# One core, attention and a gated MLP: the calls of a kernel kept in a list and issued in the order of a list schedule made in the kernel

## The chip, the cores and the metric

The kernel runs on one core of a Trainium2 chip. The metric is the device time of one execution in microseconds (us). Three runs of the kernel before took 531.16, 533.72 and 533.61 us, median 533.61 us. One more execution, the profiled one, took 530.32 us, and every row of the profile is from it.

The core has five engines that run side by side, each in the order of its own queue: TensorE (PE, matrix products; its weight loads are shown apart as PEld), VectorE (DVE), ScalarE (ACT), GpSimd (POOL) and SyncE (SP), which here only issues transfers (DMAs). An instruction starts when its engine has come to it and the semaphores that it waits for are set. So the order of the queues decides which wait ends where.

## The reference

The input is `q`, `k`, `v` of shape (4 batches, 8 heads, 768 rows, 64), and four arrays of an MLP: `w_in` (512, 1024), `w_spatial` (768, 768), `b_spatial` (768), `w_out` (512, 512). The three MLP matrices but for `w_spatial` come as 64-bit floats.

```
scores = scale * q @ k^T                              # 768 x 768 for each head
keep   = (column < n_global) or (0 <= row - column < n_local)      # 8 and 96
bias   = -slope[h] * distance                         # n_local for a far global column
a      = softmax(where(keep, scores + bias, -1e9));   a /= sum + 1e-9
x      = (a @ v), heads side by side                  # 4 x 768 x 512
h      = relu(x @ w_in);   u, v = halves of h         # 512 features each
v_n    = (v - mean(v)) / sqrt(var(v) + 1e-6)          # over the features of a row
v_s    = w_spatial @ v_n + b_spatial                  # over the 768 rows of a batch
out    = (u * v_s) @ w_out
```

Since only 96 columns to the left and 8 global ones are kept, a block of 128 rows needs two blocks of 128 columns, its own and the one before it; the global columns are put into a corner of the latter that is masked otherwise.

## The kernel before

**Steps and tokens.** The work of attention goes in 24 steps n = 0 to 23, six for each batch (b = n // 6, i = n % 6), each of 128 rows and all eight heads. Around the steps stand pieces of other work, named by tokens of a letter and two digits in a table `CFG['S']` (batch 0) or `CFG['T']` (the later batches). The letters:

- P, `prep`: transfers of q and k. In batch 0 they land straight in their places (L279, L280). From batch 1 on they are loaded into `qkraw` (L294), split into a rounded high part and the rest (L127, L123), and copied by twelve further transfers from there into `q`, `ql` and `kring` (L302, L303, L300), so that one product of 128 rows takes both parts.
- S, `scores`: for each pair of heads a product (L364 in batch 0 in plain 32-bit floats, L367 afterwards in two passes of split parts), bias and row minimum on DVE (L373), exponent on ACT (L377), reciprocal of the sums (L259, L260), and the scaling of the 128x256 probabilities on POOL (L388).
- A, `values`: transposes on PE (L421), copies or splits out of the transposes' PSUM (L50, L127, L123), the product with v (L430, from batch 1 L451), and the assembly and split of x into `xth` and `xtl` (L50, L461, L463, L127, L123). W, `prep_v`: loads and splits v.
- V, `mlp_v`: half of x @ w_in for 128 rows (L493), relu, mean and variance, and the split into `vnh` and `vnl`. U, `mlp_u`: the other half for 256 rows (L516, L517). G, `mlp_s`: the product with `w_spatial` for 256 rows (L531), plus b and times u (L533, L535), split into `gh` and `gl`. O, `mlp_o`: the product with `w_out` (L549), the copy out of PSUM (L50) and the output transfer (L551). A product of the MLP and of the later attention is made in three passes of high and low parts.
- I, Q, T, B: the set-up of `w_in` (eight tiles of 128x512), `w_out` (four), `w_spatial` (six, L242) and b. A tile of the 64-bit weights is loaded as words (L197), turned into a 32-bit float and a rest by an ACT instruction (L222) and six of DVE (L223 to L228), and split by two of POOL (L230, L231) and one of ACT.

The second digit of a token is the tile, the first is by how many batches the token lags behind the step: V15 in batch 1 is the last V of batch 0. After the last step come V15, U12, then by hand G for chunk 0, G for chunk 1 (its result in the places of `xth` and `xtl`, which are free by then), O 0, G 2, O 1, O 2.

**What sets the order.** The kernel is written in one run from top to bottom. The framework's own scheduler (the program is built with `schedule_with_timeline_sim=True`) moves instructions between the tokens and fixes the order of each queue. Tiles come from pools with rotating buffers. Of the tiles that matter below, `qkraw`, `qkhi`, `q` and `ql` have one buffer each, `kring` two columns, the probabilities `pr` ten buffers, `pth` two, `vnh` and `vnl` six each, `gh` and `gl` one each; the weight set-up takes its two intermediates from the `vnh` and `vnl` buffers and its words from the three of `u`. In PSUM the scores, the transposes and the MLP have two places each, the product with v one of two banks.

Of the kernel before, what the change touches and what calls it, by code (L numbers as in the profile page):

```python
# [23 lines left out]

CFG = {'bpos': 1, 'v0pos': 0, 'bias1': 'pppppppp', 'bias2': 'pppppppp', 'S': [['P', 'I01', 'S', 'W', 'A', 'I00'], ['P', 'S', 'W', 'T01', 'T00', 'A', 'V00', 'B00'], ['P', 'S', 'V01', 'Q00', 'Q01', 'W', 'U00', 'A'], ['V02', 'P', 'W', 'T04', 'S', 'T03', 'A'], ['P', 'S', 'W', 'A'], ['P', 'A', 'T02', 'Q02', 'V04', 'V03', 'S', 'W', 'Q03', 'T05', 'U01']], 'T': [['P', 'W', 'A', 'V15', 'U12', 'S'], ['P', 'A', 'S', 'G10', 'W'], ['P', 'W', 'A', 'S', 'O10', 'V00'], ['G11', 'P', 'A', 'S', 'V01', 'O11', 'W'], ['P', 'W', 'A', 'U00', 'G12', 'V02', 'S'], ['P', 'W', 'U01', 'A', 'S', 'V03', 'V04', 'O12']], 'END': ['V15', 'U12'], 'lead': {}, 'pre_n': 1, 'pre0': 0, 'pre1': 1, 'whi': 'a', 'wsub': 'p', 'wadd': 'p', 'wth': 'a', 'wtl': 'p', 'vhi': 'p', 'vlo': 'p', 'qhi': 'a', 'qlo': 'v', 'khi': 'a', 'klo': 'v', 'pth0': 'aaaa', 'x0h': 'aa', 'x0l': 'vv', 'pth': 'aaaa', 'xh': 'aa', 'c1': 'aa', 'xl': 'pppp', 'vnh': 'a', 'vnl': 'p', 'gm': 'pp', 'gh': 'aa', 'gl': 'pv', 'o': 'aa', 'norm0': 'pppppppp', 'norm': 'pppppppp', 'dup': 1, 'fold': '', 'xb': 1, 'div': 'a', 'rows': 'p', 'xf0h': 'a', 'xf0l': 'v', 'xdiv': 'v', 'xbh': 'a', 'xbl': 'p', 'b_rawqk': 1, 'b_ev': 3, 'b_raw': 1, 'b_pr': 10, 'b_pth': 2, 'b_c1': 3, 'b_ps_s': 2, 'b_ps_p': 2, 'b_ps_o': 2, 'b_ps_m': 2}
NLMAX = 97

# [713 lines left out]
```

## Time and profile before

| | |
|---|---|
| median of three runs | 533.61 us (531.16 to 533.72) |
| the profiled execution | 530.32 us, its span 528.5 us |
| busy PE / DVE / POOL / ACT | 474.2 / 350.6 / 325.4 / 301.9 us |
| matmuls | 3116 |
| mean granted TensorE clock | 0.97 |
| moved by DMA | 65.50 MB, 124 GB/s on average |

The profile's span starts with the first instruction and ends with the last; 1.8 us of the profiled execution lie around it. Busy times count an instruction's own duration. Matmuls overlap each other in the array, so their busy time is more than the time that they take from start to start, and a busy PE may still be slower than it could be. The chain of waits follows the work that ended last back through whatever released each step. In a row of the timeline or of a group, brackets or arrows name what ended the idle time before the instruction.

### The profile page before, as it was taken

To read this page: it belongs to the slowest core of one execution; us is meant where nothing else is said; L and a number is where in the kernel's file an instruction comes from. 1 tells how busy PE (TensorE), PEld (TensorE's weight loads), DVE (VectorE), ACT (ScalarE), POOL (GpSimd) and SP (SyncE) were. 2 spreads that over 40 slices of the span, in tenths; PEclk is the share of its full clock that TensorE was granted. 3 is DMA by queue.
4 is the path that set the end of the run, shared out by engine and by line. 5 is a ranking of instruction groups with operands and counts; after the bars stand their busy time and mean duration, and the time that the engine had idled before them with its cause. 6 is when DMAs were issued, how large, how long until landed. Compare 5 with 4: busy or idle time off the path is not lost.

```text
span 528.5 us, 9830 instructions
## 1 busy us (share of the span) xinstructions
PE 474.2 (90%) x3116; PEld 427.9 (81%) x3116; DVE 350.6 (66%) x972; ACT 301.9 (57%) x800; POOL 325.4 (62%) x450
## 2 busy tenths in 40 slices
PE   3757599898988999997989999989999999979994
PEld 2535489678977999986979899969989899869994
DVE  6899988869697585476785775767587856331210
ACT  3775478666666484666575575675475576431111
POOL 6999997866774753846662947644753757523320
PEclk9987789999999999999999999998999999989998
DMA  7993412961755755466655764655755760000002
GB/s 173 288 245 106 144 60 52 214 145 51 153 139 138 172 133 125 98 154 160 145 118 150 169 163 99 147 146 137 159 112 147 183 140 21 22 20 1 21 35 73
DMA packets 68269, 65.50 MB, mean 124 GB/s; under 512 B 6672, under 2 KB 49936, under 8 KB 68208
## 3 DMA queue, kind: packets, MB, share of 16 engines
q1 hardware_dynamic: 68208, 64.78, 49.9%
q8 instruction: 27, 0.44, 0.4%
q14 instruction: 34, 0.28, 0.2%
HBM read 29.76 MB, written 6.68 MB: 69 GB/s over the span
## 4 chain that ended last, share of the span: by engine, by line
PE 48%; DVE 17%; DMA 13%; SPq 8%; ACT 6%; issue 5%; POOL 2%; DVEq 0%; ACTq 0%; POOLq 0%
PE sps L531 13%; PE vps L493 8%; PE ups L516 8%; PE ops L549 7%; PE ops L451 4%; DVE pr L373 3%; PE pt L421 3%; DMA qkraw<-in_k_dram 3%; PE sp L367 3%; ACT pr L377 2%; DMA qkraw<-in_q_dram 2%; DMA kring<-qkraw 2%; SPq L303 2%; DVE qkraw L123 2%; SPq L300 2%
## 5 line engine op out<-in xcount | busy, mean ns | idle before, releaser
L388 POOL TENSOR_SCALAR pr<-pr,rc 128x256 f32<-128x256 f32 (+1 forms) x192 | 99.6, 537 | 23.4 <-DVE rc L260 9.1
L377 ACT ACTIVATE pr<-pr,mn 128x256 f32<-128x256 f32 (+1 forms) x192 | 92.2, 482 | 33.7 <-DVE mn L373 32.5
L421 PE MATMUL pt<-ident,pr 128*128 128x128 f32 x352 | 58.4, 280 | 14.7 <-POOL pr L388 11.6
L373 DVE CUSTOM_DVE_ANT_0 pr<-sp,bias 128x256 f32<-128x256 f32 (+1 forms) x192 | 68.1, 395 | 4.6 <-PE sp L364 1.4
L421 PEld LDWEIGHTS pt<-ident,pr 128*128 128x128 f32 x352 | 42.0, 143 | 23.9 <-POOL pr L388 16.5
L123 DVE TENSOR_TENSOR pth<-pt,pth 128x512 fp32r<-128x512 f32 (+1 forms) x72 | 46.0, 642 | 16.6 <-ACT pth L127 15.4
L535 POOL TENSOR_TENSOR g<-g,u 128x512 f32<-128x512 f32 x24 | 32.0, 1331 | 34.8 <-DVE g L533 34.7
L127 ACT ACTIVATE pth<-pt 128x512 fp32r<-128x512 f32 (+1 forms) x72 | 39.2, 558 | 23.6 <-PE pt L421 20.9
L123 POOL TENSOR_TENSOR xtl<-c,xth 128x256 fp32r<-128x256 f32 x36 | 27.3, 758 | 35.8 <-ACT xth L127 28.5
L123 POOL TENSOR_TENSOR vnl<-vr,vnh 128x512 fp32r<-128x512 f32 x24 | 31.9, 1332 | 27.6 <-ACT vnh L127 26.6
L531 PE MATMUL sps<-w_t_l,vnh 128*128 128x256 f32 x288 | 45.8, 286 | 0.0
L531 PE MATMUL sps<-w_t_h,vnh 128*128 128x256 f32 x288 | 44.9, 286 | 0.8 <-ACT u L517 0.5
L451 PE MATMUL ops<-pth,vring 128*128 128x256 f32 x264 | 41.8, 288 | 3.0 <-DVE pth L123 2.1
L461 DVE TENSOR_TENSOR c<-ops,c 64x256 f32<-64x256 f32 x72 | 30.3, 421 | 21.4 <-ACT c L50 16.6
L531 PE MATMUL sps<-w_t_h,vnl 128*128 128x256 f32 x288 | 44.4, 285 | 0.0
L364 PE MATMUL sp<-kring,q 128*128 128x256 f32 (+1 forms) x96 | 28.7, 450 | 16.8 <-DMA kring<-in_k_dram 9.9
L451 PEld LDWEIGHTS ops<-pth,vring 128*128 128x128 f32 x264 | 36.4, 192 | 5.2 <-DVE pth L123 2.8
L367 PE MATMUL sp<-kring,q 128*128 128x256 f32 (+1 forms) x144 | 38.3, 292 | 2.4 <-DMA q<-qkhi 1.2
L531 PEld LDWEIGHTS sps<-w_t_h,vnh 128*128 128x128 f32 x288 | 38.7, 191 | 1.6 <-ACT vnh L127 0.8
L531 PEld LDWEIGHTS sps<-w_t_l,vnh 128*128 128x128 f32 x288 | 39.0, 191 | 0.0
L533 DVE TENSOR_TENSOR g<-sps,b_bc 128x512 f32<-128x512 f32 x24 | 16.5, 686 | 33.8 <-PE sps L531 31.5
L531 PEld LDWEIGHTS sps<-w_t_h,vnl 128*128 128x128 f32 x288 | 38.6, 191 | 0.0
(115 smaller groups left out, 1204.4 us busy)
## 6 DMA issues: line engine op xcount, KB each, us to landing
q<-qkhi SPq DMA_DIRECT2D x72, 128.0 KB, 2.5
ql<-qkraw SPq DMA_DIRECT2D x72, 128.0 KB, 2.5
out_dram<-o SPq DMA_DIRECT2D x23, 256.0 KB, 2.6
qkraw<-in_q_dram SPq DMA_DIRECT2D x36, 128.0 KB, 3.0
qkraw<-in_k_dram SPq DMA_DIRECT2D x36, 128.0 KB, 2.9
raw<-in_v_dram SPq DMA_DIRECT2D x18, 256.0 KB, 3.2
kring<-qkhi SPq DMA_DIRECT2D x36, 128.0 KB, 2.5
kring<-qkraw SPq DMA_DIRECT2D x36, 128.0 KB, 2.5
```

Source lines behind the costliest of these rows:

```text
L123: e_lo.tensor_tensor(out=lo, in0=src, in1=hi.bitcast(F32), op=ALU.subtract)
L127: nc.scalar.activation(hi, src, AF.Copy)
L367: nc.tensor.matmul(sp[:, j], lhsT=a[:, g, j] if CFG["dup"] else a[:, h], rhs=kring[:, h, sl], start=(y == 0), stop=(y == 1))
L373: nc.vector.tensor_tensor_reduce(out=pr, in0=sp[:, j], in1=bt, scale=-scale, scalar=3e38, op0=ALU.add, op1=ALU.min, accum_out=mn[:, h:h + 1],)
L377: nc.scalar.activation(pr, pr, AF.Exp, bias=mn[:, h:h + 1], scale=-1.0, accum_out=sm[:, h:h + 1])
L388: nc.gpsimd.tensor_scalar(out=pr, in0=pr, scalar1=rc[:, h:h + 1], scalar2=1.0, op0=ALU.mult, op1=ALU.mult)
L421: nc.tensor.transpose(pt[:, c, j], probs[2 * g + j][:, c * P:(c + 1) * P], ident)
L451: nc.tensor.matmul(ops[:, j], lhsT=vring[:, order[c], g, 2 * j:2 * j + 2].rearrange("p x d -> p (x d)"), rhs=pth[:, 2 * c + j].rearrange(" ...
L493: nc.tensor.matmul(ps, lhsT=a[:, t, toks], rhs=w[:, t, FH:], start=(x == 0), stop=(x == len(passes) - 1))
L516: nc.tensor.matmul(ps[:, j], lhsT=w[:, t, f * P:(f + 1) * P], rhs=a[:, t], start=(x == 0), stop=(x == len(passes) - 1))
L531: nc.tensor.matmul(ps[:, j], lhsT=vn[b, s][x][:, f * P:(f + 1) * P], rhs=w[:, s, ts_], start=(y == 0), stop=(y == len(passes) - 1))
L549: nc.tensor.matmul(ps[:, cs], lhsT=a[:, f, x * P:(x + 1) * P], rhs=w[:, f, cs], start=(y == 0), stop=(y == len(passes) - 1))
```

## The change

The products, their number, shapes and passes, and the work of each token are those of before. Changed is how the order comes about, and where tiles lie.

**Recording.** `nc` is replaced by a `Recorder` whose engines do not issue a call but keep it (`Op`), with its token and a number. At the end `plan()` sorts them, and they are issued in that order under `tc.manual_schedule()`, which turns the framework's scheduler off. All instructions now carry the line of `Op.issue`, L35, so that they are told apart by the names of their places.

**The list schedule.** `link()` finds for each call the earlier ones whose buffers overlap its own. `cost()` gives each a duration and a time to its result by formulas. `plan()` lets the five engines run by these: an engine that becomes free takes, of the calls that are ready, the one with the lowest rank. The rank is the token's: n for values, n + 0.2 for the loads and splits of step n + 1, n + 0.5 for its scores and for every MLP token in step n; at equal rank the call written earlier comes first. POOL's instructions and the DVE instructions that touch no PSUM are never run at the same time in it.

**Places.** Instead of rotating buffers, `Slots` hands out fixed places in turn. The weight set-up's intermediates now lie in `raw0`, `raw1`, `rawh0`, `rawh1`, which are also the only places of `qkraw` and `qkhi`, and the words of `w_out` in `gh` and `gl`.

**Tokens.** `scores` and `values` are written in two halves of four heads, taken alternately (a half of A for step n, a half of S for step n + 1, and again). The table is new, and END is `V05 U02 G00 O00 G01 O01 G02 O02`, without the spare places for the second `gh` and `gl`. The constant 1e-9 that is added to the sums is put into a second column beforehand, and a `tensor_reduce` takes the place of the `tensor_scalar` (L259).

```diff
+class Engine:
+    def __getattr__(self, call):
...
+        def keep(*args, **kw):
+            self.rec.add(self, call, args, kw)
...
+def cost(op):
+    n = elements(op.writes[0])
...
+    if op.eng == "sync":
+        size = n * 4 * list(op.writes[0].ap)[0][1]
+        return 560, 2200 + size * .0035, False
...
+def plan(ops, keys, trace=None):
+    link(ops)
...
+    rank = [(keys.get(op.token[0], op.token[1]), op.num) for op in ops]
+    free = {x: 0.0 for x in ("tensor", "vector", "scalar", "gpsimd", "sync")}
...
+        x = heapq.heappop(ready[e])[1]
...
+        start[x] = t
+        free[e] = t + op.busy
+        end = t + op.late
...
+            at = t + op.busy if o.eng == e and e != "sync" else end + SLACK
+            est[s] = max(est[s], at)
...
+    return sorted(ops, key=lambda op: (start[op.num], op.num))
+
+BUFS = {"gh": 1, "gl": 1, "u": 3, "s": 2, "p": 2, "m": 2, "raw0": 1, "raw1": 1, "rawh0": 1, "rawh1": 1}
+SLACK = 200
...
-        c = work.tile([P, w], F32, name="wc", tag="vnh", bufs=6)
+        c = work.tile([P, w], F32, name="wc", tag=("raw0", "rawh0")[x % 2])
-        a = work.tile([P, w], F32, name="wa", tag="vnl", bufs=6)
+        a = work.tile([P, w], F32, name="wa", tag=("raw1", "rawh1")[x % 2])
...
-        split_weights(w_out[t * P:(t + 1) * P], w_out_h[:, t], w_out_l[:, t])
+        split_weights(w_out[t * P:(t + 1) * P], w_out_h[:, t], w_out_l[:, t], ("gh", "gl")[t % 2], t)
...
     def recip(out, sums):
-        nc.vector.tensor_scalar(out=out, in0=sums, scalar1=1e-9, scalar2=None, op0=ALU.add)
+        nc.vector.tensor_reduce(out=out, in_=sums, op=ALU.add, axis=mybir.AxisListType.X)
...
-    def mlp_s(b, c, tags=(("gh", 1), ("gl", 1))):
+    def mlp_s(b, c):
...
+            if tok == "A":
                 if more:
+                    nc.token(("P", n + 1), n + .2)
+                    qq = prep(n + 1)
+                    s = scores(n + 1, qq)
+                a = values(n)
+                for x in range(2):
+                    steps("A", a, n)
+                    if more:
+                        steps("S", s, n + 1)
...
+    for tok in CFG["END"]:
+        run(tok, B * NB, B - 1, int(tok[2]))
+    nc.off()
+    with tc.manual_schedule():
+        for op in plan(nc.ops, KEYS):
+            op.issue()
```

The token tables, before and now:

```
before S [P I01 S W A I00] [P S W T01 T00 A V00 B00] [P S V01 Q00 Q01 W U00 A] [V02 P W T04 S T03 A] [P S W A] [P A T02 Q02 V04 V03 S W Q03 T05 U01]
       T [P W A V15 U12 S] [P A S G10 W] [P W A S O10 V00] [G11 P A S V01 O11 W] [P W A U00 G12 V02 S] [P W U01 A S V03 V04 O12]
now    S [I01 A] [I00 T00 T01 A V00 B00] [T02 T03 A V01 U00] [T04 T05 A V02] [Q00 Q01 A V03 U01] [Q02 Q03 A V04]
       T [V15 U12 A] [G10 O10 A] [G11 O11 A] [G12 O12 V00 V01 U00 A] [V02 A] [V03 U01 A V04]
```

**What moves on SP, at the border of batch 0 and batch 1.** Before, SP's queue has the twelve copies for step 6 (`q`, `ql` and `kring` out of `qkhi` and `qkraw`) ahead of the last two tiles of `w_out`:

```order
L302 DMA q_1029<-qkhi 64x512 x4
L480 DMA vring_223<-in_v_dram 32x512
L325 DMA vring_223<-in_v_dram 128x512
L303 DMA ql<-qkraw 64x512 x4
L300 DMA kring<-qkhi 64x4x128
L300 DMA kring<-qkraw 64x4x128
L300 DMA kring<-qkhi 64x4x128
L300 DMA kring<-qkraw 64x4x128
L197 DMA wst<-in_moe_w_out_dram 128x1024 x2
```

Now, with q in `q_0_151` and `q_0_152` and the loads of q and k in `raw_0_114` and `raw_0_115`:

```order
L35 DMA gh_130<-in_moe_w_out_dram 128x1024
L35 DMA gl_131<-in_moe_w_out_dram 128x1024
L35 DMA raw_0_114<-in_q_dram 64x4x128 x2
L35 DMA vg<-vring_155 32x1024
L35 DMA raw_156<-in_v_dram 128x512
L35 DMA raw_0_115<-in_k_dram 64x4x128 x2
L35 DMA q_0_151<-rawh_0_153 64x512 x4
L35 DMA q_0_152<-raw_0_114 64x512 x4
L35 DMA kring_150<-rawh_0_154 64x4x128 x2
L35 DMA kring_150<-raw_0_115 64x4x128 x2
```

The last two words of `w_out` have moved ahead of all that belongs to step 6, its loads and its copies.

**What moves on PE, at the same border.** Before, the scores of step 6 (`sp`, from `kring` and `q` or `ql`) are in front of the first products with v of step 5, batch 0's last (`ops` from `pth_1060`):

```order
L367 MATMUL sp<-kring,q_1029 128x128
L367 MATMUL sp<-kring,ql 128x128
L421 MATMUL pt<-ident,pr 128x128 x8
L493 MATMUL vps<-w_in_h,xth 128x512 x2
L493 MATMUL vps<-w_in_l,xth 128x512 x4
L493 MATMUL vps<-w_in_h,xtl 128x512 x2
L430 MATMUL ops<-pth_1060,vring_223 128x256 x2
L430 MATMUL ops<-pth_1069,vring_223 128x256 x2
```

Now the products of step 5 (`ops_93`) are followed by MLP work of batch 0 (`m_132`, `m_140`: what is left of V04, then V15, U12 and the first of G10):

```order
L35 MATMUL ops_93<-pth_123,vring_112 128x256 x2
L35 MATMUL ops_93<-pth_125,vring_112 128x256 x2
L35 MATMUL m_132<-w_in_h,xtl_121 128x512 x3
L35 MATMUL m_140<-w_in_h,xth_120 128x512 x4
L35 MATMUL m_140<-w_in_l,xth_120 128x512 x4
L35 MATMUL m_140<-w_in_h,xtl_121 128x512 x4
L35 MATMUL m_132<-xth_120,w_in_h 128x256 x4
L35 MATMUL m_132<-xtl_121,w_in_h 128x256 x4
```

The first scores of step 6 (`s_102`, `s_105`) come 15 matmuls of 512 columns, 48 of U and ten of G behind the last product with v:

```order
L35 MATMUL m_140<-w_t_h,vnh_148 128x256
L35 MATMUL m_140<-w_t_h,vnh_158 128x256
L35 MATMUL s_102<-kring_150,q_0_151 128x128
L35 MATMUL s_102<-kring_150,q_0_152 128x128
L35 MATMUL s_105<-kring_150,q_0_151 128x128
L35 MATMUL s_105<-kring_150,q_0_152 128x128
L35 MATMUL m_132<-w_t_h,vnh_160 128x256
```

So the scores of step 6 have moved from ahead of batch 0's last values to well behind them.

More of the change, by code (lines that the diff above doesn't have):

```diff
@@ L2 @@
+import heapq
 from contextlib import ExitStack
@@ new lines, with __init__, tile @@
+class Slots:
+    def __init__(self, pool, words, bufs):
+        self.pool, self.words, self.bufs, self.have, self.turn = pool, words, bufs, {}, {}
+    def tile(self, shape, dtype, name=None, tag=None, bufs=None):
+        tag = tag or name
+        bufs = self.bufs.get(tag, bufs or 2)
+        n = 1
+        for x in shape[1:]:
+            n *= x
+        x = self.turn.get(tag, 0)
+        self.turn[tag] = x + 1
+        place = f"{tag}_{x % bufs}"
+        key = place, dtype == F32R
+        if key not in self.have:
+            t = self.have[key] = self.pool.tile([P, self.words.get(tag, n)], F32, name=place, tag=place)
+            places[t[:].tensor.name] = place
+        t = self.have[key][:, 0:n]
+        if dtype != F32:
+            t = t.bitcast(dtype)
+        dims = " ".join("abcdef"[:len(shape) - 1])
+        return t if len(shape) == 2 else t.rearrange(f"p ({dims}) -> p {dims}", **dict(zip("abcdef", shape[1:])))
@@ new lines, with extent @@
+SIZE = {BF16: 1}
+seen = {}
+places = {}
+def extent(ap):
+    t = ap.tensor
+    key = t.name, ap.offset, tuple(tuple(x) for x in ap.ap), str(ap.dtype)
+    if key not in seen:
+        u = SIZE.get(ap.dtype, 2)
+        row = 1
+        for x in t.shape[1:]:
+            row *= x
+        row = row * SIZE.get(t.dtype, 2) // u
+        p0, f0 = divmod(ap.offset, row)
+        bits = 1
+        for stride, n in reversed([tuple(x) for x in ap.ap][1:]):
+            part = bits
+            if stride:
+                bits = 0
+                for x in range(n):
+                    bits |= part << (x * stride * u)
+        unit = (1 << u) - 1
+        seen[key] = places.get(t.name, t.name), p0, p0 + ap.ap[0][1], (bits * unit) << (f0 * u)
+    return seen[key]
@@ L553, in attn_then_spatial_gating_kernel, with run, steps @@
     NAMES = {"V": mlp_v, "U": mlp_u, "G": mlp_s, "O": mlp_o, "I": setup_w_in, "Q": setup_w_out, "T": setup_w_t, "B": setup_b}
-    END = CFG["END"]
-    def at(key, f, *args):
-        lead = CFG["lead"].get(key, 0)
-        if not lead:
-            return f(*args)
-        with tc.high_priority(offset=lead):
-            return f(*args)
+    def run(tok, n, b, j):
+        nc.token((b, tok[0], j), n + .5)
+        NAMES[tok[0]](b, j)
+    def steps(kind, f, n):
+        nc.token((kind, n), n + (.0 if kind == "A" else -.5))
+        next(f, None)
```

312 lines of the change are left out of this document (241 added, 71 removed).

## The prediction

> **What bounds the kernel now.** I read the page first, then busy times by stretches, then the chain of waits for the pace of each kind of matmul.
>
> ```profile
> span 528.5 us, 9830 instructions
> PE 474.2 (90%) x3116; PEld 427.9 (81%) x3116; DVE 350.6 (66%) x972; ACT 301.9 (57%) x800; POOL 325.4 (62%) x450
> PE   3757599898988999997989999989999999979994
> DVE  6899988869697585476785775767587856331210
> POOL 6999997866774753846662947644753757523320
> ```
>
> PE is the engine to look at over most of the span, but in the first five or six slices (13.2 us each) DVE and POOL are full and PE is not. Then the stretches; behind each engine's busy time stands its count, then the granted clock, the DMA share and GB/s:
>
> ```profile
> 0.00:66.00 66.00, 38.85 (x142) 28.48 (x142) 58.25 (x168) 37.25 (x103) 60.50 (x75) 0.87 0.73 191
> 66.00:80.50 14.50, 14.23 (x70) 12.45 (x71) 11.64 (x31) 10.07 (x28) 13.81 (x18) 0.88 0.24 72
> 80.50:121.50 41.00, 37.82 (x225) 33.03 (x225) 33.20 (x90) 29.79 (x78) 31.19 (x41) 1.00 0.58 133
> 121.50:145.00 23.50, 21.37 (x164) 20.09 (x164) 18.97 (x46) 14.64 (x40) 15.71 (x21) 1.00 0.45 102
> 145.00:464.00 319.00, 307.06 (x2150) 283.29 (x2149) 217.97 (x623) 198.12 (x533) 188.31 (x283) 0.99 0.55 132
> 464.00:528.50 64.50, 54.91 (x372) 50.58 (x370) 10.59 (x19) 12.06 (x22) 15.88 (x15) 0.94 0.09 31
> ```
>
> Busy PE time counts overlapped matmuls too long, so I take the paces of undisturbed runs in the chain of waits (start, us, what, how many):
>
> ```profile
> 75.63 1.73 PE ops L430 x8
> 179.02 0.87 PE pt L421 x8
> 440.58 2.75 PE vps L493 x12
> 444.27 2.86 PE ups L516 x24
> 479.14 17.28 PE sps L531 x144
> ```
>
> That is 0.216 us for a record of a plain 32-bit product of 256 columns, 0.109 for a transpose, 0.229 for 512 columns and 0.12 for 256 in a split product. The 3116 matmuls come to 447 us of work by these (352 transposes 38; 564 of 512 columns 129; the plain products of batch 0, 38; the rest at 0.11 to 0.12, 242). So 81 us of the span are lost on PE. By the counts of each stretch they lie so: 41 of 66 us up to 66.0, 2 up to 80.5, 5 up to 121.5, 3 up to 145, 19 of 319 in the middle, 12 of 64.5 at the end. The number and shape of the matmuls stay, so the change can only move these 81 us.
>
> **The start.** What fills DVE and POOL there is the split of the weights beside the first softmaxes (groups of the first 132 us on DVE; a line's and a tile's own rows for minimum, median and maximum in ns and first and last start):
>
> ```profile
> L228 DVE SCALAR_TENSOR_TENSOR wm<-wst,wc 128x512 f32<-128x512 uint32 x12 | 15.0, 1258 | 0.2
> L225 DVE SCALAR_TENSOR_TENSOR wa<-wc,wa 128x512 int32<-128x512 int32 x12 | 14.0, 1176 | 0.0
> L225 DVE SCALAR_TENSOR_TENSOR wa<-wc,wa x12: 675/806/2315, 12.4 to 123.7; 128x512 int32<-128x512 int32 x12
> L231 POOL TENSOR_TENSOR w_in_l<-wa,wm x8: 1266/1366/1727, 23.4 to 79.2; 128x512 fp32r<-128x512 f32 x8
> L231 POOL TENSOR_TENSOR w_out_l<-wa,wm x4: 1274/1299/1712, 96.6 to 131.5; 128x512 fp32r<-128x512 f32 x4
> ```
>
> The eighth tile of `w_in` is done at 79.2 + 1.3 = 80.5 us, when POOL has been busy for 60.50 + 13.81 = 74.3 and DVE for 69.9 us. None of these instructions is removed. In the new POOL order the eighth tile stands behind about 2 us more POOL work than before, so I put it at 82 (at best 76, if POOL's 6 idle us vanish; at worst 90). What does change is how far PE gets before it must have that tile: before it had done about 37 us of work by 80.5; in the new order 46 us of work stand ahead of the first matmul that reads the tile. From there to the last product with v of batch 0 are 26 us of work; with the 4.8 lost by 41 us that the third stretch shows, 30. That is 82 + 30 = 112 us. Before it was here:
>
> ```profile
> L430 PE MATMUL ops<-pth,vring x24: 377/379/381, 105.5 to 121.1; 128*128 128x256 f32 x24
> L451 PE MATMUL ops<-pth,vring x8: 283/283/283, 129.3 to 135.9; 128*128 128x256 f32 x8
> ```
>
> So 121.5 before. But then comes a wait that is new. Step 6's q and k can be loaded only after the last tile of `w_out` has left the shared places, and SP has them behind it. The price of a step's q and k is seen in SP's timeline (the first and last of eleven copies in a row, then two loads), in DVE's half of a split, and in the page's issues (us to landing):
>
> ```profile
> 219.81 0.56 SPq L302 DMA_DIRECT2D q<-qkhi  x1
> 226.28 0.63 SPq L300 DMA_DIRECT2D kring<-qkraw  x1
> 227.02 1.23 SPq L294 DMA_DIRECT2D qkraw<-in_q_dram  x2
> L123 DVE TENSOR_TENSOR qkraw<-qkraw,qkhi 128x512 fp32r<-128x512 f32 x6 | 5.6, 927 | 0.0
> q<-qkhi SPq DMA_DIRECT2D x72, 128.0 KB, 2.5
> qkraw<-in_q_dram SPq DMA_DIRECT2D x36, 128.0 KB, 3.0
> ```
>
> Four loads 2.5 and landing 3.0, the split about 1.5 (DVE's 0.93 behind ACT's half, for which I take 0.6), twelve copies 7.7 (eleven from 219.81 to 226.91), landing 2.5: 17 in a row, some 15 where the parts for q and for k overlap. PE has 10.4 us of filler there (15 x 0.229 and 58 x 0.12). I take a wait of 5; ends are 0 (the places come free early) and 12 (the fourth tile as late behind batch 0 as before). Up to step 6's last product with v there are 22 us of work, 94.2 in all, so that it comes at 112 + 22 + 5 = 139 us. Before, 94.2 us of work were done at 144.8. Allowing 1 us for MLP work that runs in the wait, the start gives **-7 us** (ends -16 and +5).
>
> [...]
>
> **The middle.** 300 us of work took 319. What PE waits for in the table of waits (total, times, longest), the exponents on the page, and what SP waits for:
>
> ```profile
> PE pt L421 <- POOL pr L388: 11.6, 9, 4.9
> PE ops L451 <- DVE pth L123: 2.1, 2, 1.5
> L377 ACT ACTIVATE pr<-pr,mn 128x256 f32<-128x256 f32 (+1 forms) x192 | 92.2, 482 | 33.7 <-DVE mn L373 32.5
> SPq L551 <- ACT o L50: 91.9, 14, 33.8
> SPq L300 <- PE sp L367: 40.7, 9, 7.5
> ```
>
> A transpose that waits for its probabilities is what halves and ranks are to cover; I expect the jitter of that kind to fall from 19 to about 4 us. Against it stands the spread of work. `q` and `ql` have one place each, so the copies for step n + 1 start only when the scores of n are done: 7.7 + 2.5, and the scores of eight heads in two halves, about 5 (eight exponents of the row here are 3.9, and they come behind the first product), give some 15 us for a step at the least. In the new order the work between the last values of successive steps is about 20, 30.3, 14.9, 11.4, 15.7 and 15.4 us in a batch: V15 and U12, recorded early, and V00, V01, U00 are bunched. The stretch of 11.4 falls 3.6 short, and each near 15 by up to 0.5; over two and a half batches about 10 us. So 14 are lost for 19: **-4 us** (ends -9, if the copies get ahead in the fat stretches, and +14 at a cycle of 17).
>
> **The end.** The waits that I can see, in the timeline:
>
> ```profile
> 466.42 0.77 ACT L50 ACTIVATE c<-ops 64x256 f32<-64x256 f32 x2 [0.89 <-PE ops L451]
> 469.50 0.93 PE L493 MATMUL vps<-w_in_h,xth 128*128 128x512 f32 x2 [2.88 <-ACT xth L127]
> 512.71 0.63 ACT L127 ACTIVATE gh<-g 128x512 fp32r<-128x512 f32 x1 [3.67 <-POOL g L535]
> 513.38 0.69 DVE L123 TENSOR_TENSOR gl<-g,gh 128x512 fp32r<-128x512 f32 x1 [2.06 <-ACT gh L127]
> ```
>
> The wait of 2.88 for the last x has some 2 us of V and U work in front of it now: -1.7. With G and O of a chunk back to back, each O must wait for the last G half's way through DVE, POOL, ACT and DVE, 510.4 to 514.1 = 3.7 us here; twelve of its matmuls read the first half and cover 12 x 0.229 = 2.7, so about +0.3 three times and up to +1 each. The half clock that the 0.94 of this stretch holds may go with the wait: -1. **-2 us** (ends -4 and +3). The sums' `tensor_reduce` stands for a `tensor_scalar` of DVE, 48 in all:
>
> ```profile
> L259 DVE TENSOR_SCALAR rc<-sm 128x4 f32<-128x4 f32 x15 | 5.9, 390 | 0.7 <-ACT pr L377 0.7
> ```
>
> Half to twice this is between 9 us less and 19 more of DVE work, under an engine that idles 178: 0, and at most +2 in the start, where it doesn't idle.
>
> **Sum.** 528.5 - 7 - 4 - 2 = 515.5 us of span, 517.3 with the 1.8 around it. The profiled execution was 3.3 below its median; from the median the same -13 gives 520.6. I say 518.
>
> **Rivals.** *Start not shorter:* DVE and POOL set the eighth tile and the fourth of `w_out`; if the attention of batch 0 waits for the same two engines, 46 us of work cannot be reached by 82 and the last values come at 121.5 as before. Then the wait of 5 is added to 22 of work: 148.5, less the 1 us of work in the wait, +3 for -7: 528.5 + 3 - 4 - 2 + 1.8 = 527. For it: both engines are at 8 or 9 in slices two to six. Against: the old order left DVE 10.6 and POOL 6.2 of the 80.5 us idle. *Slower, the copies' cycle:* SP works in order, and the row of 33.8 us shows it standing behind an output that is not ready; one such output ahead of the copies makes the cycle longer than 15. At 18 the stretches of 14.9, 11.4, 15.7 and 15.4 fall short by 14.6 together, 39 in 2.7 batches, and with the jitter 43 are lost for 19: 528.5 + 24 - 7 - 2 + 1.8 = 545 us. It decides above a cycle of some 16.5, where gains and losses are even. In favour: `q`, `ql` and the loads' places are single. Against: before, SP stood 40.7 us at L300 for scores that had yet to free `kring`, so it had time left with the same places. *The loss only moves:* with 447 us of fixed work any order of these buffers may lose about the same; 531 to 536. *Larger gain:* the jitter goes, and fat stretches let SP run ahead; start -16, middle -9, end -4 are the best ends together, 501.
>
> [...]
>
> **How the numbers follow.** Forecast 0.46 (507 to 525), start not shorter 0.18, slower by the cycle 0.14, loss only moved 0.10, larger gain 0.12 (below 507). The range that leaves out most of the slow case and the far end of the fast one is 500 to 535. A change under 0.5% (2.7 us; the three runs lie 2.6 apart) can't be told: 530.9 to 536.3 counts as same. Faster: 0.46 + 0.12 + 0.14 of the second + 0.03 of the fourth = 0.75; same 0.04 of the second + 0.05 of the fourth = 0.09; slower 0.14 + 0.02 of the fourth = 0.16.
>
> **What would show it.** Right: the last product with v of batch 0 near 112 us, PE idle of some 5 us before the first scores of step 6, stalls on `q` only in the stretch of step 3 of a batch, and no wait near 3 us for the last x. Wrong: the eighth tile of `w_in` after 90, or copies of successive steps 18 us apart while PE waits for them. That the order on the chip isn't the one shown would void all of it.

## The result and the profile after

The change makes the kernel slower: 558.59 us (557.03 to 561.15, four runs) for 533.39; the ratio is 1.0486, 95% interval 1.0432 to 1.0540. The forecast was 518 us, its range 500 to 535. Three executions among all runs below were slow ones and are not compared: one of the kernel before (1597 us), one of `slack` (560.5) and one of `plan_even_late` (781.5; without it the median of 535.9 would be 535.5).

The page of the changed kernel, the lines that answer to those of before:

```profile
span 559.4 us, 9755 instructions
PE 493.3 (88%) x3116; PEld 432.1 (77%) x3116; DVE 349.6 (62%) x974; ACT 306.9 (55%) x800; POOL 322.1 (58%) x450
PE   4787879995987998998889999999889999899995
DVE  5856989985575666477755655578776582751110
POOL 4875889876634655266664655377756465253221
PEclk9858999997897998999998999999999999999998
```

DVE and POOL are busy for as long as before, in a span that is 31 us longer, and PE has the same 3116 matmuls (their busy time, which counts overlaps, is 493.3 us for 474.2). So nothing became more work; PE waits more. To say where, both spans are cut at the last product with v of step 5 (batch 0's last), of step 6 and of step 23. Before, then the change (columns as in the prediction's table of stretches):

```profile
0.00:121.10 121.10, 90.49 (x434) 73.59 (x435) 102.69 (x285) 76.92 (x206) 105.10 (x133) 0.92 0.62 158
121.10:135.90 14.80, 13.32 (x98) 12.42 (x97) 14.55 (x36) 8.87 (x25) 10.37 (x11) 1.00 0.19 46
135.90:466.10 330.20, 317.57 (x2229) 292.87 (x2228) 224.04 (x639) 204.98 (x550) 195.49 (x295) 0.99 0.55 132
466.10:528.50 62.40, 52.86 (x361) 49.05 (x359) 9.34 (x16) 11.15 (x20) 14.45 (x13) 0.94 0.09 32
```

```profile
0.00:117.90 117.90, 93.54 (x424) 72.05 (x425) 92.18 (x257) 71.03 (x184) 89.01 (x119) 0.90 0.43 122
117.90:151.80 33.90, 26.73 (x171) 24.79 (x170) 21.87 (x50) 13.62 (x37) 23.96 (x28) 0.85 0.58 148
151.80:498.10 346.30, 318.95 (x2157) 286.50 (x2157) 224.78 (x650) 210.08 (x557) 192.76 (x288) 0.98 0.50 128
498.10:559.40 61.30, 54.10 (x369) 48.75 (x367) 10.77 (x19) 12.21 (x22) 16.40 (x16) 0.98 0.08 28
```

Behind these marks lies different work in each kernel, so what counts is the time lost on PE: the stretch less its matmuls at the prediction's paces (0.216, 0.109, 0.229 and 0.12 us). Below, "start", "border", "middle" and "end" are this loss up to step 5, to step 6, to step 23, and to the last matmul. Before it is 47.5, 1.9, 20.1 and 5.7 us; now it is 45.6, 12.0, 45.9 and 3.9. The loss of the middle has more than doubled, and that alone is 26 of the 31 us.

What PE waits for in the whole span, the first rows of the table of waits:

```profile
PE s L35 <- DVE mn L35: 12.5, 18, 2.1
PE s L35 <- DMA kring<-in_k_dram: 7.7, 1, 7.7
PE m L35 <- DVE ev L35: 5.8, 3, 2.4
PE s L35 <- DMA kring<-raw: 5.6, 1, 5.6
PE ops L35 <- DVE c L35: 4.6, 10, 0.9
```

The wait for the copies of q and k, on which my slower rival rested, is there once in the kernel (5.6 us, at the border); the 7.7 us are at the start, as before. Most of the others are short, many, and end on DVE, an engine that is idle 38% of the time. In the middle alone, first rows before (135.9 to 466.1 us):

```profile
PE pt L421 <- POOL pr L388: 4.4, 3, 2.3
PE ops L451 <- DVE pth L123: 2.1, 2, 1.5
```

and with the change (151.8 to 498.1 us), with the last row:

```profile
PE s L35 <- DVE mn L35: 8.1, 13, 1.3
PE m L35 <- DVE ev L35: 5.8, 3, 2.4
PE ops L35 <- DVE c L35: 4.6, 10, 0.9
PE ops L35 <- DVE pth L35: 2.9, 6, 0.7
PE p L35 <- POOL pr L35: 0.6, 1, 0.6
```

All rows together, PE waits 12 us in the middle before, 2.3 of them on DVE, and 27 us now, 22.6 of them on DVE. (The loss is larger than the waits, since a wait is counted only from the end of the last matmul's record, and that is 0.28 us long at a pace of 0.12.) The wait of transposes for POOL's probabilities (`pr`) has fallen, from 4.4 to 0.6 us.

One of the waits on DVE: rows of ACT and POOL, DVE's timeline, and then PE's row:

```profile
209.50 0.63 ACT L35 ACTIVATE rawh<-raw 128x512 fp32r<-128x512 f32 x1 [1.71 <-DMA raw<-in_k_dram]
209.82 1.31 POOL L35 TENSOR_TENSOR vring<-raw,vring 128x512 fp32r<-128x512 f32 x1
```

```profile
210.16 1.51 DVE L35 TENSOR_TENSOR raw<-raw,rawh 128x512 fp32r<-128x512 f32 x1 [2.10 <-ACT rawh L35]
211.59 1.77 DVE L35 TENSOR_TENSOR c<-ops,c 64x256 f32<-64x256 f32 x4
213.40 0.69 DVE L35 TENSOR_TENSOR ev<-m,b_bc 128x512 f32<-128x512 f32 x1
214.00 0.41 DVE L35 CUSTOM_DVE_ANT_0 pr<-s,bias 128x256 f32<-128x256 f32 x1
214.34 0.08 DVE L35 DVE_READ_ACCUMULATOR2_ANT mn<- 128x1 f32 x1
```

```profile
214.14 0.73 PE L35 MATMUL m<-w_out_h,gh 128*128 128x512 f32 x2 [2.42 <-DVE ev L35]
```

PE wants a PSUM place that holds a finished G. DVE reads it at 213.40, behind the split of a later step's q or k (1.51 us; `cost()` has 72 + 1.04 x 512 ns = 0.60) and four additions for x (1.77; `cost()` has 4 x 0.34 = 1.35). By the schedule's durations the two end 1.3 us earlier. That is half of the 2.42: the split, which the queue has in front, had itself kept DVE idle for 2.10 us, until k had landed and ACT had made its half. The same three instructions stand in front of a wait at 294 and at 414 us.

Other durations are further off. The statistics of a row are costed by the elements that they write, six, at 0.076 us; a split of q or k is 0.60 in the formula. The rows:

```profile
L35 DVE BATCH_NORM_STATS2 st<-ev x24: 680/694/696, 75.6 to 504.9; 128x6 f32<-128x512 f32 x24
L35 DVE TENSOR_TENSOR c<-ops,c x144: 404/424/429, 148.9 to 500.7; 64x256 f32<-64x256 f32 x144
L35 DVE TENSOR_TENSOR raw<-raw,rawh 128x512 fp32r<-128x512 f32 x36 | 33.3, 933 | 15.0 <-ACT rawh L35 14.4
```

24 x 0.62 = 15 us, 144 x 0.10 = 14 us (0.44 from start to start) and 36 x 0.33 = 12 us: about 41 us of DVE's 350 are not in these durations, and its queue is fixed. Of the 12, however, some 9 are what 16 of the splits take beyond 0.69 us, 15 of them behind POOL, and that `plan()` does have, in its way, as its rule that the two never run together:

```profile
L35 DVE TENSOR_TENSOR raw<-raw,rawh x36: 677/694/1779, 127.8 to 453.7; 128x512 fp32r<-128x512 f32 x36
```

In the trace 20 of the 36 splits take 0.68 to 0.72 us. The other 16 take 0.95 to 1.78, and 15 of these end 0.54 to 0.55 us after the POOL instruction that was running when they began, as the one above does (POOL until 211.13, the split until 211.67). I read that as a split that waits for POOL and whose duration contains the wait. It is not so beside every POOL instruction: the splits at 262.02 and 383.88 take 0.69 us within one that scales probabilities (0.92 us, from 261.95 and from 383.81). The additions, which read PSUM, show no such wait: 50 of the 144 lie for more than half of their time beside a POOL instruction, and none takes over 0.43 us. So some 32 us of DVE are unknown to the schedule altogether.

### The profile page after: what moved, and what is told of

Read it like the earlier page. It is cut to its first block, busy times and chain, and to the rows that moved or that the text cites. A ratio compares the mean times of both kernels' runs of the same rounds, so it can differ in the third digit from the quotient of the medians.

```text
span 559.4 us, 9755 instructions
## 1 busy us (share of the span) xinstructions
PE 493.3 (88%) x3116; PEld 432.1 (77%) x3116; DVE 349.6 (62%) x974; ACT 306.9 (55%) x800; POOL 322.1 (58%) x450
## 4 chain that ended last, share of the span: by engine, by line
PE 52%; DVE 19%; POOL 8%; ACT 7%; DMA 5%; issue 5%; SPq 3%; POOLq 0%; ACTq 0%; DVEq 0%
PE m L35 34%; DVE c L35 8%; PE ops L35 7%; PE s L35 7%; PE p L35 4%; DVE pr L35 4%; SPq L35 3%; POOL pr L35 3%; DMA raw<-in_k_dram 2%; DVE ev L35 2%; ACT c L35 2%; DVE pth L35 1%; DVE raw L35 1%; ACT pr L35 1%; DMA u<-in_moe_w_in_dram 1%
## 5 line engine op out<-in xcount | busy, mean ns | idle before, releaser
L35 POOL TENSOR_SCALAR pr<-pr,rc 128x256 f32<-128x256 f32 (+1 forms) x192 | 96.6, 525 | 37.0 <-DVE rc L35 26.9
L35 ACT ACTIVATE pr<-pr,mn 128x256 f32<-128x256 f32 (+1 forms) x192 | 92.1, 481 | 35.1 <-DVE mn L35 34.6
L35 PE MATMUL s<-kring,q 128*128 128x256 f32 (+1 forms) x384 | 79.1, 336 | 27.1 <-DVE mn L35 12.5
L35 PEld LDWEIGHTS s<-kring,q 128*128 128x128 f32 x384 | 63.2, 211 | 38.9 <-DVE mn L35 19.1
L35 DVE CUSTOM_DVE_ANT_0 pr<-s,bias 128x256 f32<-128x256 f32 (+1 forms) x192 | 69.0, 397 | 30.5 <-PE s L35 27.1
L35 PE MATMUL ops<-pth,vring 128*128 128x256 f32 x352 | 75.5, 335 | 13.9 <-DVE c L35 4.6
L35 DVE TENSOR_TENSOR c<-ops,c 64x256 f32<-64x256 f32 x144 | 60.7, 422 | 29.7 <-ACT c L35 24.1
L35 PEld LDWEIGHTS ops<-pth,vring 128*128 128x128 f32 x352 | 55.2, 198 | 26.0 <-ACT pth L35 7.4
L35 ACT ACTIVATE pth<-p 128x512 fp32r<-128x512 f32 (+3 forms) x96 | 52.5, 561 | 37.9 <-PE p L35 37.2
L35 PE MATMUL p<-ident,pr 128*128 128x128 f32 x352 | 61.3, 283 | 4.2 <-POOL pr L35 4.0
L35 DVE TENSOR_TENSOR pth<-p,pth 128x512 fp32r<-128x512 f32 (+1 forms) x72 | 45.4, 643 | 30.9 <-ACT pth L35 29.7
L35 POOL TENSOR_TENSOR xtl<-c,xth 128x256 fp32r<-128x256 f32 x36 | 29.9, 832 | 49.9 <-ACT xth L35 46.0
L35 PEld LDWEIGHTS p<-ident,pr 128*128 128x128 f32 x352 | 43.3, 145 | 13.6 <-POOL pr L35 9.0
L35 POOL TENSOR_TENSOR ev<-ev,u 128x512 f32<-128x512 f32 x24 | 31.1, 1296 | 37.4 <-DVE ev L35 35.9
L35 PE MATMUL m<-w_t_h,vnh 128*128 128x256 f32 x288 | 47.3, 292 | 1.3 <-ACT u L35 1.3
L35 PE MATMUL m<-w_t_h,vnl 128*128 128x256 f32 x288 | 48.2, 289 | 0.0
L35 PE MATMUL m<-w_t_l,vnh 128*128 128x256 f32 x288 | 45.7, 288 | 0.0
L35 POOL TENSOR_TENSOR vnl<-ev,vnh 128x512 fp32r<-128x512 f32 x24 | 31.8, 1327 | 23.3 <-ACT vnh L35 21.9
L35 ACT ACTIVATE ev<-m 128x512 f32<-128x512 f32 (+1 forms) x49 | 28.6, 587 | 30.0 <-PE m L35 28.8
L35 ACT ACTIVATE c<-ops 64x256 f32<-64x256 f32 x72 | 27.3, 379 | 29.0 <-PE ops L35 27.9
L35 DVE TENSOR_TENSOR raw<-raw,rawh 128x512 fp32r<-128x512 f32 x36 | 33.3, 933 | 15.0 <-ACT rawh L35 14.4
L35 PEld LDWEIGHTS m<-w_t_h,vnh 128*128 128x128 f32 x288 | 40.0, 195 | 1.8 <-ACT u L35 1.7
```

What stands on the lines that cost most here:

```text
L35: getattr(self.real, self.call)(*self.args, **self.kw)
```

## The experiments

Each run is compared with runs of the kernel before on the same chip, whose medians are 531 to 533 us; ratios are to these, with 95% intervals. In the table stand the median and, from the one profiled execution, the four losses. An edit is against the changed kernel unless it says otherwise.

| kernel | us | start | border | middle | end |
|---|---|---|---|---|---|
| before | 533 | 47.5 | 1.9 | 20.1 | 5.7 |
| the change | 558.6 | 45.6 | 12.0 | 45.9 | 3.9 |
| fw_order | 547.2 | 47.4 | 3.6 | 33.9 | 8.4 |
| own_places | 552.1 | 44.8 | 9.6 | 39.5 | 3.9 |
| bn_cost | 554.8 | 43.0 | 14.2 | 41.2 | 3.7 |
| meas_cost | 570.3 | 55.2 | 21.4 | 31.2 | 7.1 |
| noport | 574.3 | 57.8 | 6.5 | 54.4 | 3.5 |
| meas_noport | 558.7 | 57.0 | 3.3 | 37.1 | 7.0 |
| slack | 551.9 | 43.6 | 9.6 | 35.6 | 8.4 |
| fw_table | 549.7 | 46.1 | 1.9 | 39.4 | 8.3 |
| fw_whole | 544.3 | 46.2 | 3.6 | 31.9 | 8.3 |
| comb | 556.6 | 53.8 | 5.1 | 40.6 | 7.0 |
| before_T | 548.3 | 47.4 | 1.9 | 37.3 | 5.6 |
| fw_even | 534.6 | 49.1 | 2.4 | 24.8 | 9.2 |
| fw_even_whole | 537.2 | 47.3 | 2.9 | 23.9 | 9.2 |
| plan_even | 555.7 | 40.3 | 11.6 | 45.8 | 2.6 |
| plan_even_late | 535.9 | 40.2 | 12.4 | 23.8 | 2.7 |
| hybrid3 | 541.9 | 49.7 | 6.1 | 25.0 | 7.9 |

**fw_order: the order or what it orders.**

```diff
-    with tc.manual_schedule():
-        for op in plan(nc.ops, KEYS):
-            op.issue()
+    for op in nc.ops:
+        op.issue()
```

> The recorded calls, places, halves and token table of the changed kernel, but issued as written and ordered by the framework's own scheduler, as before the change. Theory A (the list schedule's order is bad, because its durations are shorter than the measured ones: row statistics on DVE at 0.08 us against 0.69 in the trace, an addition out of PSUM at 0.34 against 0.45 from start to start): the places and tables do no harm, so 525 to 540 us, and PE loses some 20 us between the work of step 6 and that of step 23, where it now loses 46. Theory B (fixed places, halves and tables cost the time, whatever the order): 550 us or more.

547.2 us (ratio 1.0284, 1.0230 to 1.0339): between both. So 11 of the 25 us are the list schedule's order, and some 14 belong to the calls themselves: places, halves or tables.

**own_places.** The w_out split's intermediates in the places of `ev` and of the loaded v.

```diff
-        c = work.tile([P, w], F32, name="wc", tag=("raw0", "rawh0")[x % 2])
+        out = tag[0] == "g"
+        c = work.tile([P, w], F32, name="wc", tag="ev" if out else ("raw0", "rawh0")[x % 2], bufs=3)
-        a = work.tile([P, w], F32, name="wa", tag=("raw1", "rawh1")[x % 2])
+        a = work.tile([P, w], F32, name="wa", tag="raw" if out else ("raw1", "rawh1")[x % 2], bufs=1)
```

> The changed kernel, but the intermediates of the w_out split lie in the places of ev and of the loaded v instead of those that the loads of q and k need; the list schedule is the same and makes its order anew. Theory C (the border of batch 0 and 1 loses its 12 us to the shared places): 547 to 551 us, the 5.7 us idle before the first scores of step 6 gone. Theory A: the wait moves, since the 46 us of the middle are lost step by step: 555 to 560 us.

552.1 us (1.0376, 1.0327 to 1.0425), between both forecasts. The copies come early, but the border's loss goes only from 12.0 to 9.6; the wait for them is replaced by shorter ones. The middle gains too, without having been touched: a new order is a new draw. Theory C explains little.

**bn_cost and meas_cost: durations.** The first edit is one line; the second corrects the other durations named in its expectation, too.

```diff
     elif op.call == "bn_stats":
-        t = 70 + 1.04 * n
+        t = 70 + 1.28 * elements(src)
```

> The changed kernel with one duration of the list schedule corrected: row statistics (24 on DVE) at 0.73 us instead of 0.08. Theory A: this is the largest single error, about 15 us of DVE over the span, a third of its part lies in front of something that PE waits for: 545 to 554 us. Theory B and C: 557 to 561 us.

> The changed kernel with all durations of the list schedule near to what the trace of the changed kernel has from start to start (row statistics 0.73, halves out of PSUM 0.40 on ACT and 0.45 on DVE, split of q and k 0.9 on DVE, normalisation 0.55, a transfer's issue 0.64, small DVE instructions 0.18 to 0.22, exponents 0.49 for 0.57). Theory A: the waits of PE in the middle fall from 46 to some 25 us, 530 to 545 us in all. Theory B: 555 us or more.

bn_cost 554.8 us (1.0427, 1.0357 to 1.0497), just outside the forecast of theory A; 4.7 us of the middle are gone. meas_cost 570.3 us (1.0718, 1.0657 to 1.0779), worse than the change and by the sum in theory B's range. Yet its middle is 31.2 for 45.9, the way that theory A says, if not to its 25; start and border lost 19 us more and hid that.

**noport, meas_noport, slack.** In the first, `plan()` may run DVE and POOL together; the second adds the durations of meas_cost; the third sets `SLACK` to 700 ns.

```diff
-        return t, t + 90, True
+        return t, t + 90, False
...
-    return t, t + 90, not one
+    return t, t + 90, False
```

> The changed kernel, but its list schedule lets POOL and DVE work at the same time; durations as they were. Theory A2 (the start is lost because the schedule keeps the two engines apart, which the chip does not do: in the profile before both are over 85% busy at once): the start, up to the work of step 6, comes some 8 us earlier than with the change, 546 to 552 us. [...]

> Both at once: the measured durations, and POOL and DVE allowed together (with the contended DVE durations lowered from 0.9 to 0.7 us, since contention is no longer modelled otherwise). With measured durations alone the middle fell from 45 to 31 us lost, but the start rose from 58 to 77. Theory A2: the start returns to 50 to 58 and the middle stays near 31: 535 to 545 us. [...]

> The changed kernel with one number changed: a result is counted on 0.7 us after it is due instead of 0.2 us, for every step from one engine to another. Theory E (the order is too tight: each result that comes a few tenths late stops an engine that works in order, and nothing is between): the middle loses 30 us instead of 45, 540 to 550 us. Theory B (not the order): 557 us or more. If the start is lost as with the measured durations, the sum can be 560 while the middle still falls.

noport 574.3 us (1.0799, 1.0673 to 1.0926), where theory A2 had 546 to 552. Start and border, which were to come 8 us earlier, lose 64.3 us for 57.6, and without the rule the middle loses 54.4. A2 takes two engines that are busy at once for two that run side by side. The splits of q and k above speak against that: 15 of the 36 end 0.54 to 0.55 us after the POOL instruction that they began beside.

meas_noport 558.7 us (1.0506, 1.0460 to 1.0551), above the 535 to 545 of theory A2: the middle falls to 37.1. The start stays at 57.0, but the border falls from meas_cost's 21.4 to 3.3, so the two together are 60.3 for 76.6, close to the change's 57.6. It fits that meas_cost counts the waiting for POOL twice, in 0.9 us for a split and in the rule. But this run changes durations and rule at once, so that is argued and not shown.

slack 551.9 us, one run and so without an interval: the middle falls by 10 and start and border by 2 each; the end takes 4.5 back.

**fw_table and fw_whole: what the calls cost under the framework's order.** One word moved, `['A', 'V15', 'U12']`; and the halves undone:

```diff
                 for x in range(2):
                     steps("A", a, n)
+                for x in range(2):
                     if more:
                         steps("S", s, n + 1)
```

> The recorded calls under the framework's scheduler (547.2 us), with one word moved in the token table: A ahead of V15 and U12 at the start of a batch, as the table had it before the change. There PE stood 15.0 us in four waits, up to 8.3, for the last x of a batch. Theory B2 (of what is left between 547 and 532 with the framework's order, the table is the cause): 533 to 538 us, that wait below 4 us. Theory B3 (the fixed places are): 544 to 548 us.

> The recorded calls under the framework's scheduler, with its own table, but values and scores written one after the other as a whole instead of in alternating halves. Theory B4 (halves: a half of values waits on one PE queue behind a half of scores): 535 to 542 us. Theories B2 and B3: 545 to 551 us.

549.7 us (1.0337, 1.0278 to 1.0396) and 544.3 us (1.0225, 1.0190 to 1.0260). The one word gains nothing: the border is 1.7 us better, the middle 5.5 worse, and the waits for an x that it was to shorten are still four, of 15.0 us together. The halves are worth 3 us, and the middle stays above 31 in both.

**fw_T and fw_T_whole: the old table.** `CFG['T']` as before the change, the second without halves.

> The recorded calls under the framework's scheduler (547.2 us), with the later batches' token table as before the change, so that G, O and U of the batch behind are spread over all six steps instead of standing in steps 1 to 3. Theory B2 (table): the waits for an x or its copies in the last two steps of a batch, 5 to 7 us in each, find filler: middle from 34 to some 22 us lost, 534 to 540 us. Theory B3 (places) and B4 (halves): 544 to 550 us.

> Both of these undone, so that of the change only the fixed places, the start's table, the end without spare places and the constant in the sums are left, under the framework's scheduler. If table and halves are the whole difference: 530 to 536 us. Theory B3 (the fixed places): 542 us or more.

562.3 and 574.9 us, and neither tells about the table alone. In the old table V00 is written ahead of G11 and G12. With fixed places it takes over the place of the batch behind, and those two G read the next batch's tile, that is, they wait for it and compute something else. This shows why the new table is bunched: with places handed out in written order, V00 must come after G12, while the pools before allowed it ahead.

**comb: three repairs at once** (own_places, bn_cost, `SLACK` 400).

> The changed kernel with its list schedule and three repairs together: other places for the w_out intermediates (alone -6.5 us), row statistics at 0.73 us (alone -4), and results counted on 0.4 us after they are due (0.7 alone: -2.4). Theory A and E (the order is too tight and partly on wrong durations; the parts add up): 543 to 549 us. Theory B (a floor is set by table, halves and places): 549 us or more. In no case under 540.

556.6 us (1.0473, 1.0397 to 1.0548): single gains of 6.5, 4 and 7 (slack, at 700 instead of 400) do not add.

**before_T, fw_even, plan_even, fw_even_whole: the table.** before_T is the kernel before with the MLP tokens in the change's steps; the others have a table as even as fixed places allow:

```diff
-'T': [['P', 'W', 'A', 'V15', 'U12', 'S'], ['P', 'A', 'S', 'G10', 'W'], ['P', 'W', 'A', 'S', 'O10', 'V00'], ['G11', 'P', 'A', 'S', 'V01', 'O11', 'W'], ['P', 'W', 'A', 'U00', 'G12', 'V02', 'S'], ['P', 'W', 'U01', 'A', 'S', 'V03', 'V04', 'O12']]
+'T': [['P', 'W', 'V15', 'U12', 'A', 'S'], ['P', 'W', 'G10', 'O10', 'A', 'S'], ['P', 'W', 'G11', 'O11', 'A', 'S'], ['P', 'W', 'G12', 'O12', 'V00', 'V01', 'U00', 'A', 'S'], ['P', 'W', 'V02', 'A', 'S'], ['P', 'W', 'V03', 'U01', 'A', 'V04', 'S']]
```

```diff
-'T': [..., ['G12', 'O12', 'V00', 'V01', 'U00', 'A'], ['V02', 'A'], ['V03', 'U01', 'A', 'V04']]
+'T': [..., ['G12', 'O12', 'A', 'V00'], ['V01', 'U00', 'A', 'V02'], ['A', 'V03', 'U01', 'V04']]
```

> The kernel before, pools, scheduler and all, with one edit: the later batches' token table puts the MLP tokens into the steps where the change has them (G and O of the batch behind in steps 1 to 3, V00, V01 and U00 also in step 3, little in 4, 5 and 0). Theory B2 (the bunched table is what the structure costs): 540 to 550 us, with waits in the last two steps of a batch and the first. Theory B3 (the fixed places cost it, not the table): 529 to 536 us.

> The recorded calls with fixed places under the framework's scheduler (547.2 us), and a token table that spreads the MLP as far as fixed places allow: V00 must be written after G12, since it takes the first of the six places of v_n; so V00 moves behind A in step 3, V01, U00 to step 4, U01 behind A in step 5. Theory B2: 537 to 543 us. Theory B3: 545 to 550 us.

> The changed kernel with its list schedule (558.6 us) and the same spread table, nothing else. Theory B2: the thin stretches of 11 to 15 us are filled, 545 to 552 us. Theory A or E (the order's tightness is the whole loss): 556 to 561 us.

> The spread table, the framework's scheduler and values and scores written as a whole (alone 544.3 for 547.2). If table and halves are what the structure costs, both gains add: 533 to 540 us. Theory B3: 543 us or more.

before_T 548.3 us (1.0281, 1.0203 to 1.0359): the bunched table alone costs the old kernel 15 us, 17 of its middle. fw_even 534.6 us (1.0012, 0.9977 to 1.0048): with the table spread, fixed places, halves and new start cost nothing in the sum that can be told. fw_even_whole 537.2 us (1.0085, 1.0050 to 1.0120): the halves' gain does not add. plan_even 555.7 us (1.0423, 1.0337 to 1.0509): under the list schedule the same table is worth 3 us. For the same calls, the schedule's order is now 21 us behind the framework's, though its start is 9 us better.

**plan_even_late: durations again, where they matter.** plan_even with meas_cost's durations for the calls of step 6 and later, the change's own for the start.

> The list schedule with the spread table (555.7 us, 46 us lost in the middle), and the measured durations for every call of step 6 and later; the start keeps the durations that it has, with which it lost 40 us, 9 less than under the framework's scheduler. Theory A (wrong durations are what makes the list schedule's middle bad): the middle falls to 24 to 30 us lost, as with the framework's order (25), and the sum is 533 to 543 us. Theory E2 (the greedy order itself, for any durations): middle 35 or more, 545 us or more.

535.9 us (1.0089, 1.0060 to 1.0117). The start and the border are as in plan_even; the middle, plan_even first and then this kernel:

```profile
146.10:487.50 341.40, 317.10 (x2122) 284.32 (x2123) 223.94 (x648) 204.65 (x554) 192.27 (x285) 0.98 0.51 130
```

```profile
146.90:467.50 320.60, 309.66 (x2133) 280.96 (x2133) 220.87 (x649) 205.22 (x555) 193.23 (x287) 0.99 0.54 140
```

Same calls, 20.8 us less for the same matmuls but some ten. And plan_even's waits on DVE for a PSUM place,

```profile
PE s L35 <- DVE mn L35: 9.2, 15, 1.2
PE m L35 <- DVE ev L35: 8.1, 7, 2.5
```

are 6.2 us in twelve waits for the first in plan_even_late, and the second is not among its rows, which go down to 1.1 us. The greedy order is about as good as the framework's (23.8 and 24.8, though the latter is from fw_even's slowest execution, 538.6 us) once its durations are near the chip's. Theory A holds for the middle, E2 falls.

Could the 22 us be a lucky order? Among the seven list schedules with the old durations, or with the statistics alone corrected, the middle ranges from 35.6 to 54.4. But three pairs differ in the durations above all, and each gains in the middle: the change and meas_cost 14.7, noport and meas_noport 17.3, plan_even and plan_even_late 22.0. The edit corrects durations of ACT, POOL and SP too; what DVE's share is was not separated, beyond the 4.7 of bn_cost.

**hybrid3: each order where it lost less.** fw_even's calls; steps 0 to 3 and all behind the last step in the list schedule's order, the rest in the framework's.

> The spread table and fixed places, with each scheduler where it lost less: the calls of steps 0 to 3 in the list schedule's order, those from there to the last step in the framework's, those after the last step in the list schedule's again. By the losses of the two parents (start 40 for 49, end 3 for 9 of 535 us) 520 to 526 us, faster than the kernel before; if the parts don't fit at their seams, 527 to 535 us.

541.9 us (1.0198, 1.0137 to 1.0259). That is more than both forecasts. The parts don't fit: the start's gain of 9 is lost again by step 5, and the end keeps 7.9. Losses of parts are not independent.

No version beats the kernel before. plan_even_late with w_out's intermediates elsewhere, for its border of 12.4, was not tried.

## Why the prediction was wrong, point by point

**The sum.** By its own marks: 94.2 us of work were done at 144.8 before and at 151.8 now, +7 where I had -7. The middle took 346.3 us for 319, +27 for -4. The end took 61.3 for 64.5, -3 for -2.

**The step that failed** is one sentence on the middle: "I expect the jitter of that kind to fall from 19 to about 4 us". It rose to 46. Two things are wrong in it. First, "that kind", transposes that wait for their probabilities, was 4.4 us of the middle's 12 us of waits and not the whole loss of 19; the 11.6 that I showed are of the whole span. This kind did fall, to 0.6. Second, I put the waits that the new order brings at nothing: those on DVE went from 2.3 to 22.6 us. I took for granted that a list schedule leaves small waits only, and did not hold `cost()` against rows of the kernel before:

```profile
L499 DVE BATCH_NORM_STATS2 st<-vr 128x6 f32<-128x512 f32 x5 | 3.3, 681 | 0.5 <-ACT vr L495 0.5
468.13 0.87 DVE L463 TENSOR_TENSOR c<-ops,c 64x256 f32<-64x256 f32 x2
```

681 ns for statistics where `cost()` has 76, and 0.87 us for two additions where it has 0.68, were enough to see it. The term's losing end of +14 was the copies' cycle alone; for the order itself it had none. Three pairs of runs put 15 to 22 us of the middle on the durations.

**The thin stretches** had about the right size, but not for the reason that I gave. I had 3.6 us for a stretch of 11.4; between the last values of steps 11 and 12, and of 17 and 18, they took 14.2 and 13.8 us, 2.8 and 2.5 lost. PE's waits there end on ACT (`xth` 1.5 and 1.2 us, `u` 0.5 each) and none on a copy, so the size was luck. More was lost in the stretches of 15.4, between the last values of the second and third step of a batch: 7.7, 5.4 and 2.6 us, where I had 0.5 at most; two of the three waits of the kind shown lie there. I also charged 10 us for the table and let the jitter pay for it; before_T shows its price with nothing to pay for it: 17 us. Why the table had to be bunched, the fixed places of v_n, I did not see.

**The start.** I put the eighth tile of `w_in` at 82 us, and the last products of batch 0 at 112. POOL's row:

```profile
L35 POOL TENSOR_TENSOR w_in_l<-rawh,ev x4: 1264/1312/1433, 30.7 to 92.8; 128x512 fp32r<-128x512 f32 x4
```

The tile came at 94, past 90, which I had named as a sign of being wrong; the products came at 117.9, since about 50 us of work were done ahead of the tile instead of 46. The gain was 3 us, not 9. I had taken POOL as full. In the new order it is not:

```profile
0.00:66.00 66.00, 48.60 (x177) 35.55 (x178) 45.70 (x161) 38.06 (x106) 44.90 (x71) 0.84 0.61 166
```

44.9 us for 60.5 before, and DVE 45.7 for 58.25. What leaves them idle there was not tested.

**DVE and POOL at once.** I read POOL's 74.3 us and DVE's 69.9 within 80.5 as two engines that run side by side, as theory A2 does, and put no price on the rule of `plan()` in the start. Busy times can't be read so. In the trace of before, 17 of the 24 instructions of L225 and L228 take 0.76 to 2.31 us, and each of them ends 0.54 to 0.55 us after one of POOL's; one of them, and the POOL instruction that it began beside:

```profile
44.30 2.31 DVE L225 SCALAR_TENSOR_TENSOR wa<-wc,wa 128x512 int32<-128x512 int32 x1
43.79 2.28 POOL L123 TENSOR_TENSOR w_t_l<-wst,w_t_h 128x768 fp32r<-128x768 f32 x1
```

The other seven take 0.67 to 0.69 us, six of them beside POOL too. So DVE's busy time holds time spent behind POOL, as in the long splits above, and the two sums don't tell how far the engines worked together.

**The border** had the wait that I named, at the price that I gave: loads from 118.86 on, the last copies at 133.50, and PE's row

```profile
118.86 1.21 SPq L35 DMA_DIRECT2D raw<-in_q_dram  x2
133.50 1.26 SPq L35 DMA_DIRECT2D kring<-raw  x2
```

```profile
136.01 1.12 PE L35 MATMUL s<-kring,q 128*128 128x128 f32 x4 [5.57 <-DMA kring<-raw]
```

17.1 us from the first load to the first score, 17 in a row in my sum, 5.6 for the 5 of the wait. But 12.0 were lost, not 5. The clock of this stretch is 0.85, where it was 1.00 before, and it is the matmuls behind the wait that run slower:

```profile
136.00:142.00 6.00, 5.99 (x28) 5.99 (x29) 2.99 (x20) 4.02 (x17) 2.80 (x5) 0.50 0.47 137
142.00:146.00 4.00, 4.00 (x30) 4.00 (x30) 1.37 (x3) 1.01 (x3) 2.81 (x7) 0.81 0.71 191
```

6 us at 0.50 and 4 at 0.81 are some 3.8 us lost, to which my sum gave nothing. The 0.50 came with PE's wait of 5.57 us: in windows of 1 us the clock is 1.00 up to 133, 0.50 from 134 to 143 and 1.00 again from 144. Six of G's products take 1.48 us from 141.13 and 0.87 from 143.60. What sets the clock was not tested.

**The rivals.** "Slower, the copies' cycle" has the sign and, at 545, half the size, but by luck: copies stopped PE once. "The start not shorter" was nearly true (117.9 for 121.1). The chance of 0.16 for slower was too low, since I asked of one mechanism only what it could cost, and of the new order only what it could save.

**The end** is as forecast: no wait near 3 us for the last x, and the end's loss is 3.9 for 5.7. The half clock that I counted with stands in this row of before, right behind the wait of 2.88:

```profile
470.50:472.50 2.00, 2.00 (x6) 1.52 (x6) 0.00 (x0) 0.00 (x0) 0.00 (x0) 0.50 0.00 0
```

Now PE's longest wait there is 0.8 us, and the clock of the stretch is 0.98 for 0.94.

**A slip** changes nothing: 14 lost for 19 is -5 and not -4.

## What to carry to other kernels

Before trusting a schedule that is made from a cost formula, lay the formula beside the profile's rows, instruction kind by instruction kind, and ask of a long duration whether it contains a wait for another engine (the splits here: 0.68 to 0.72 us, and up to 1.78 behind POOL); an engine that is a third idle (here DVE, 38%) still stops the bound one when its queue is fixed in the wrong order (22.6 us of PE's waits in the middle). Fixed places handed out in written order limit how work can be spread, so a table that pools allowed may no longer be possible. A correction to one part of a tight schedule can be hidden by a new order elsewhere: compare stretch by stretch, not by the total.

## What the runs showed that I had not expected

An addition over 64 partitions and 256 columns out of PSUM takes longer on DVE than the bias and minimum over 128 partitions and as many columns: in the timeline above four take 1.77 us, 0.44 each, while the latter follow each other at 0.34 (214.00, 214.34). Whether shape or a wait for the one before makes it, was not tried. And a rule that I had thought needless was worth something: with DVE and POOL allowed together and the durations of the change, noport is 16 us slower (574.3 for 558.6), and in the trace of the change 15 of DVE's 36 splits of q and k end 0.54 to 0.55 us after a POOL instruction.
